# Splitting the last batch's spatial and output products into two 64-row tiles

## The chip, the cores and the metric

The kernel runs on one core of a Trainium2 chip. The time is the device time of one execution in microseconds; the number that counts is the median of several runs. The engines are named as in the profile: PE (TensorE; PEld are its weight loads), DVE (VectorE), ACT (ScalarE), POOL (GpSimd) and SP (SyncE, which issues the DMAs).

## The reference

Causal attention over 4 batches, 12 heads, 448 positions and 64 dimensions, and behind it a gated MLP per batch:

```python
scores = scale * np.matmul(q, k.transpose(0, 1, 3, 2))      # then causal mask, softmax
x = matmul(attn, v) laid out as (batch, 448, 768)
h = gelu(x @ w_in)                                          # 768 -> 1024
u, v = h[..., :512], h[..., 512:]
v_n = (v - mu) / np.sqrt(var + 1e-06) * g_ln
v_s = np.einsum('ts,bsd->btd', w_sg, v_n) + b_sg[None, :, None]
out = x + (u * v_s) @ w_out                                 # 512 -> 768
```

## The kernel before

Attention goes by head pairs, 24 of them, six per batch. For each pair PE computes scores (line 433, plain f32, tiles of 64 rows and 64 columns), DVE masks and finds the maxima (448), ACT takes exponentials (456); then transposes, and the products with v (line 526, tiles of 128 rows and 64 columns). Behind the six pairs of a batch comes `mlp(b)`, whose products are all made by the helper `group` (line 573): it gets a PSUM bank `ps` and a list of weight and moving operands, and issues one matmul each (line 581), in blocks of `CUT` = 3. The operands are of type f32r, split into a high and a low part, so each block of three is high x high, high x low and low x high for one slice of the contraction. All of these matmuls use the full array of 128 rows.

`mlp(b)` has four parts, named in the `od.ctx` keys:

- v: four token tiles, 18 products of 512 columns each (the last tile 12), then gelu, mean and variance, and the normalised `vn` (for the last, half-sized tile `vn3`);
- u: four feature groups of 18 products of 448 columns, gelu into `uT`;
- s: four groups of 11 products of `vn` with w_sg; DVE multiplies by `gcol` and adds `bB` (line 671), POOL multiplies by `uT` (675), ACT and POOL split the result into two halves `gT` (677, 678);
- o: six output groups of 12 products of `gT` with w_out; POOL has put the residual x into `res` (691), DVE adds the bank to it (704) and SP stores it (708 in the last batch, where each group goes out alone and the last one in two halves).

There are eight PSUM banks, shared by everything that PE writes; `bank(tag)` asks for one. Nothing is scheduled at run time: every operation is recorded with a number in `Order.add`, and the table `ORDER` (line 66) is the sequence in which they are written out. Each engine works through its own part of that sequence in order.

Of the kernel before, what the change touches and what calls it, by code (L numbers as in the profile page):

```python
# [13 lines left out]
ALU = mybir.AluOpType  # L14
# [50 lines left out]
FULL = 128, 128  # L65
ORDER = (
# [161 lines left out]
def attention_gated_mlp(ctx: ExitStack, tc: tile.TileContext, qk, vP, w_in, g_ln, w_sgT, b_sg, w_out, out):  # L228
# [338 lines left out]


    vn = {}
    uT = {}  # L570
    gT = {}

    def group(ps, m, n, mms, r):

        per = n / 2400 + (0.02 if n == 512 else 0.0135)
        cut = CUT
        for a in range(0, len(mms), cut):
            def go(a=a):
                for k in range(a, min(a + cut, len(mms))):
# [188 lines left out]
```

## Time and profile before

| | us |
|---|---|
| median of 3 runs | 340.32 (339.68 to 341.67) |
| profiled execution, its own time | 341.12 |
| its span | 339.3 |
| PE busy | 326.6 |
| DVE busy | 258.3 |
| ACT busy | 197.2 |
| POOL busy | 174.1 |

The span is what the profiler sees between the first and the last instruction; the execution's own time holds a little more around it. Matmuls are pipelined, so a matmul's record is longer than the step from one to the next, and the step is read from a run of equal matmuls: its length, less one record, by the number of steps. PEld overlaps PE.

### The profile page before, as it was taken

What the parts mean: (1) busy time and instruction counts of PE and PEld (TensorE: products, weight loads), DVE (VectorE), ACT (ScalarE), POOL (GpSimd) and SP (SyncE); (2) the same over time, 40 slices, a digit from 0 to 9 for tenths busy, and PEclk for the clock granted to TensorE, in tenths of its full rate; (3) what the DMA queues carried; (4) which work ended last, traced back from release to release, by engine and by line L of the source; (5) the groups of instructions that cost most, each with busy time, mean ns of one, the idle gap of its engine ahead of it and who ended that gap; (6) DMA issues with size and microseconds to landing.
All of it is one profiled execution on the core that took longest, in us unless ns stands there. A gap on an engine that the chain in (4) does not pass through costs nothing.

```text
span 339.3 us, 7630 instructions
## 1 busy us (share of the span) xinstructions
PE 326.6 (96%) x2614; PEld 267.5 (79%) x2615; DVE 258.3 (76%) x762; ACT 197.2 (58%) x658; POOL 174.1 (51%) x225
## 2 busy tenths in 40 slices
PE   3999998999999999999999999999999999999994
PEld 2666675868988878878898878877988988889994
DVE  4899976999999988889699767798877521577512
ACT  3999987996667658476645727384645301344300
POOL 4457666787588843223236608402407833352670
PEclk9999999999999999999999999999999999999998
DMA  7887789592584889857769368557342651201003
GB/s 227 321 251 269 251 247 275 150 322 87 126 228 136 243 218 260 231 143 167 174 187 268 101 208 266 111 155 212 83 115 40 209 141 55 108 2 54 0 29 136
DMA packets 31255, 57.75 MB, mean 170 GB/s; under 512 B 3312, under 2 KB 15344, under 8 KB 31216
## 3 DMA queue, kind: packets, MB, share of 16 engines
q1 hardware_dynamic: 31216, 57.26, 58.1%
q8 instruction: 21, 0.34, 0.4%
q14 instruction: 18, 0.15, 0.2%
HBM read 33.39 MB, written 7.08 MB: 119 GB/s over the span
## 4 chain that ended last, share of the span: by engine, by line
PE 83%; ACT 6%; DVE 4%; DMA 4%; issue 1%; SPq 1%; DVEq 0%; ACTq 0%
PE m L581 63%; PE o L526 10%; PE s L433 8%; ACT P L456 5%; DMA rd<-rT 2%; DVE s L448 1%; DMA g<-in_w_out_dram 1%; DMA qk<-in_qk_dram 1%; ACT B L507 1%; ACT vn L368 1%; PE s L470 1%; DVE vn L372 1%; PE tx L500 1%; PE ty L500 1%; DVE vn L370 0%
## 5 line engine op out<-in xcount | busy, mean ns | idle before, releaser
L456 ACT ACTIVATE P<-s,ngm 64x64 f32<-64x64 f32 (+3 forms) x240 | 100.9, 434 | 35.3 <-DVE ngm L448 28.5
L448 DVE CUSTOM_DVE_ANT_0 s<-s,mask 128x192 f32<-128x192 f32 (+3 forms) x192 | 77.2, 438 | 11.2 <-PE s L433 10.0
L581 PE MATMUL m<-win,x 128*128 128x512 f32 (+1 forms) x264 | 65.7, 399 | 0.1
L581 PE MATMUL m<-x,win 128*128 128x448 f32 x288 | 61.5, 367 | 0.0
L581 PE MATMUL m<-g,wout 128*128 128x448 f32 x288 | 61.3, 368 | 0.0
L581 PEld LDWEIGHTS m<-x,win 128*128 128x128 f32 x288 | 53.7, 188 | 5.2
L581 PEld LDWEIGHTS m<-g,wout 128*128 128x128 f32 x288 | 53.5, 188 | 5.1 <-ACT P L456 0.2
L581 PEld LDWEIGHTS m<-win,x 128*128 128x128 f32 (+1 forms) x264 | 46.7, 183 | 11.9 <-POOL win L375 0.2
L433 PE MATMUL s<-qk 64*64 64x64 f32 (+5 forms) x768 | 46.6, 375 | 6.4 <-DMA qk<-in_qk_dram 5.1
L456 ACT ACTIVATION_READ_ACCUMULATOR P<-s,ngm 128x1 f32 (+1 forms) x240 | 49.9, 208 | 0.0
L433 PEld LDWEIGHTS s<-qk 64*64 64x64 f32 x768 | 30.4, 140 | 23.4 <-issue 10.1
L526 PE MATMUL o<-B,vraw 128*64 128x64 f32 (+4 forms) x672 | 45.3, 291 | 0.3 <-DVE B L505 0.3
L526 PEld LDWEIGHTS o<-B,vraw 128*64 128x64 f32 x672 | 33.0, 137 | 13.5 <-issue 5.5
L488 DVE STREAM_TRANSPOSE P<-P 128x1024 f32<-128x1024 f32 x32 | 38.9, 1228 | 2.1 <-DMA B<-P 1.8
L691 POOL TENSOR_TENSOR res<-x 128x448 f32<-128x448 f32 x24 | 27.6, 1166 | 21.5 <-DMA out_dram<-res 21.3
L581 PE MATMUL m<-wsg,vn 128*128 128x448 f32 x176 | 38.1, 367 | 0.0
L562 POOL TENSOR_TENSOR x<-xt,x 128x448 fp32r<-128x448 f32 x24 | 27.5, 1148 | 15.2 <-ACT x L561 14.9
L581 PEld LDWEIGHTS m<-wsg,vn 128*128 128x128 f32 x176 | 32.7, 188 | 2.9
L704 DVE TENSOR_TENSOR res<-m,res 128x448 f32<-128x448 f32 (+1 forms) x25 | 14.7, 600 | 19.0 <-PE m L581 19.0
L592 ACT ACTIVATE tmp<-tmp 128x448 f32<-128x448 f32 (+2 forms) x32 | 18.9, 601 | 16.4 <-DVE tmp L590 16.4
L625 POOL TENSOR_TENSOR mv<-mv,mhalf 128x1 f32<-128x1 f32 (+1 forms) x16 | 10.0, 626 | 35.8 <-DVE mv L623 35.7
L675 POOL TENSOR_TENSOR tmp<-tmp,g 128x448 f32<-128x448 f32 x16 | 18.3, 1148 | 17.5 <-DVE tmp L671 17.4
(77 smaller groups left out, 395.2 us busy)
## 6 DMA issues: line engine op xcount, KB each, us to landing
B<-P SPq DMA_DIRECT2D x64, 256.0 KB
qk<-in_qk_dram SPq DMA_DIRECT2D x24, 448.0 KB
vn<-in_w_in_dram SPq DMA_DIRECT2D x12, 512.0 KB
vraw<-in_vP_dram SPq DMA_DIRECT2D x24, 256.0 KB
rb<-rd SPq DMA_DIRECT2D x24, 224.0 KB
out_dram<-res SPq DMA_DIRECT2D x9, 448.0 KB
g<-in_w_out_dram SPq DMA_DIRECT2D x16, 192.0 KB
rd<-rT SPq DMA_DIRECT2D x48, 32.0 KB
```

The source lines that it names most:

```text
L433: nc.tensor.matmul(out=s[z][bk].t[64 * h:64 * h + 64, col:col + n], lhsT=qk_.t[r, 0, q0:q0 + 64], rhs=qk_.t[r, 1, k0:k0 + n], start=True, ...
L448: nc.vector.tensor_tensor_reduce(out=o, in0=i, in1=mk, scale=-0.125, scalar=3e38, op0=ALU.add, op1=ALU.min, accum_out=ngm[ib[z]][c][0:m])
L456: act(n, lambda c=c, m=m, k0=k0, n=n, bk=bk, col=col, off=off, kc=kc, i=i, z=z: nc.scalar.activation(out=P[i][0:m, off:off + n], in_=s[z][ ...
L488: dve(PW, lambda z=z: nc.vector.transpose(A[ia][:, :, :, z, :].rearrange("p g t k -> p t g k"), P[ib[z]]), Pk[z] + [kp], Ak, 1.105)
L526: nc.tensor.matmul(out=dst(o.t[r]), lhsT=vr.t[:, c, r], rhs=src(z), start=first and n == 0, stop=last and n == len(lst) - 1)
L562: pool_tt(S, lambda: nc.gpsimd.tensor_tensor(out=y.t[:, S + 64:], in0=x.t, in1=f(y.t)[:, 0:S], op=ALU.subtract), [x, y], [(y, 1)])
L581: nc.tensor.matmul(out=ps.t[0:l().shape[1], 0:n], lhsT=l(), rhs=rr(), start=(k == 0), stop=(k == len(mms) - 1))
L592: act(n, lambda: nc.scalar.activation(out=z(), in_=z(), func=AF.Tanh, scale=GS * GC), [], [t], True)
L625: od.add("pool", 0.46, lambda mv=mv, m=m: nc.gpsimd.tensor_tensor(out=mv.t[0:m, 1:2], in0=mv.t[0:m, 1:2], in1=mhalf[0:m], op=ALU.pow), ["s ...
L675: pool_tt(S, lambda z=z, u=u: nc.gpsimd.tensor_tensor(out=z(), in0=z(), in1=u.t, op=ALU.mult), [u], [t])
L691: pool_tt(S, lambda rr=rr, x=x, k=k: nc.gpsimd.tensor_tensor(out=rr.t[:, k, :], in0=f(x.t)[:, 0:S], in1=f(x.t)[:, S + 64:], op=ALU.add), [ ...
L704: dve(hi - lo, lambda rr=rr, ps=ps, z=z, lo=lo, hi=hi: nc.vector.tensor_tensor(out=rr.t[:, z, lo:hi], in0=ps.t[:, lo:hi], in1=rr.t[:, z, l ...
```

## The change

Only in the last batch (`b == B - 1`), the s groups and five of the six o groups get a second PSUM bank `ps2`. `group` then issues each product as two matmuls: rows 0 to 63 of both operands into `ps`, rows 64 to 127 into `ps2`, each in its own row tile. The sums of the two banks are brought together by DVE: in an s group the old instruction reads `ps`, and a second one of the same kind adds `ps2` times `gcol`; in an o group an additional add takes `ps2` into `res` ahead of the old one. The sixth o group is left whole. The added operations give new numbers, and the table `ORDER` is another one throughout.

```diff
+    378, 390, 76, 385, 77, 341, 379, 719, 724, 726, 725, 79, 734, 467, 399, 732, 727, 495, 736, 759, 760, 765, 763,
...
-    def group(ps, m, n, mms, r):
+    def group(ps, m, n, mms, r, ps2=None):
...
                     l, rr = mms[k]
-                    nc.tensor.matmul(out=ps.t[0:l().shape[1], 0:n], lhsT=l(), rhs=rr(), start=(k == 0), stop=(k == len(mms) - 1))
+                    for o, h in ((ps, slice(0, 128)),) if ps2 is None else ((ps, slice(0, 64)), (ps2, slice(64, 128))):
+                        nc.tensor.matmul(out=o.t[0:l().shape[1], 0:n], lhsT=l()[h], rhs=rr()[h], start=(k == 0),
+                                         stop=(k == len(mms) - 1))
...
-            pe(per * len(mms[a:a + cut]), go, rd, [ps])
+            pe(per * len(mms[a:a + cut]), go, rd, [ps] + [ps2] * (ps2 is not None), FULL if ps2 is None else (64, 128))
...
         for dc in range(FC):
-            ps = bank("m")
+            ps, ps2 = bank("m"), bank("m") if b == B - 1 else None
             od.ctx = ("s", b, dc)
...
-            group(ps, 128, S, mms, r)
+            group(ps, 128, S, mms, r, ps2)
...
                 out=z(), in0=ps.t[:, 0:S], scalar=gcol[:, dc:dc + 1], in1=bB, op0=ALU.mult, op1=ALU.add),
                 [ps, "gb"], [t])
+            if ps2 is not None:
+                dve(S, lambda z=z, ps2=ps2, dc=dc: nc.vector.scalar_tensor_tensor(
+                    out=z(), in0=ps2.t[:, 0:S], scalar=gcol[:, dc:dc + 1], in1=z(), op0=ALU.mult, op1=ALU.add),
+                    [ps2, "gb"], [t])
...
         for mc in range(KC):
-            ps = bank("m")
+            ps, ps2 = bank("m"), bank("m") if b == B - 1 and mc < KC - 1 else None
...
-            group(ps, 128, S, mms, r)
+            group(ps, 128, S, mms, r, ps2)
...
+            if ps2 is not None:
+                dve(S, lambda rr=rr, ps2=ps2, z=z: nc.vector.tensor_tensor(
+                    out=rr.t[:, z, :], in0=ps2.t[:, 0:S], in1=rr.t[:, z, :], op=ALU.add), [ps2], [(rr, z)])
```

What stands where, at three places. First PE in the last batch, where the products with w_sg begin. In the names, `x` and `win` are a u group, `wsg` and `vn` an s group. In the kernel before, blocks of the two kinds alternate:

```order
L581 MATMUL m_3736<-x_3636,win_87 128x448 x3
L581 MATMUL m_3740<-x_3509,win_87 128x448 x3
L581 MATMUL m_3740<-x_3511,win_87 128x448 x3
L581 MATMUL m_3740<-x_3631,win_87 128x448 x3
L581 MATMUL m_3843<-wsg_89,vn_3680 128x448 x3
L581 MATMUL m_3740<-x_3636,win_87 128x448 x3
L581 MATMUL m_3747<-x_3511,win_87 128x448 x3
```

In the kernel after, on the same engine at the same place:

```order
L582 MATMUL m_3833<-x_3494,win_87 128x448 x3
L582 MATMUL m_3833<-x_3600,win_87 128x448 x3
L582 MATMUL m_3833<-x_3636,win_87 128x448 x3
L582 MATMUL m_3854<-wsg_89,vn_3685 128x448
L582 MATMUL m_3856<-wsg_89,vn_3685 128x448
```

All u groups now stand ahead of the first s group, and from there the two banks (3854 and 3856) take turns, call by call, through the s groups and five o groups; the last o group, with full products, stands at the end.

Second DVE in the last batch, from the last s groups to the first output adds; `tmp` is the gated value, `res` the output. Before:

```order
L671 SCALAR_TENSOR_TENSOR tmp_3922<-m_3843,gcol_84,bB_85 128x448
L671 SCALAR_TENSOR_TENSOR tmp_3934<-m_3907,gcol_84,bB_85 128x448
L704 TENSOR_TENSOR res_3678<-m_3943,res_3678 128x448
L704 TENSOR_TENSOR res_3997<-m_3959,res_3997 128x448
L704 TENSOR_TENSOR res_3684<-m_3951,res_3684 128x448
```

After:

```order
L673 SCALAR_TENSOR_TENSOR tmp_3963<-m_3925,gcol_84,bB_85 128x448
L677 SCALAR_TENSOR_TENSOR tmp_3963<-m_3927,gcol_84,tmp_3963 128x448
L673 SCALAR_TENSOR_TENSOR tmp_3977<-m_3933,gcol_84,bB_85 128x448
L677 SCALAR_TENSOR_TENSOR tmp_3977<-m_3935,gcol_84,tmp_3977 128x448
L710 TENSOR_TENSOR res_4058<-m_3983,res_4058 128x448
L713 TENSOR_TENSOR res_4058<-m_3981,res_4058 128x448
L710 TENSOR_TENSOR res_4060<-m_3999,res_4060 128x448
```

Each result now takes two instructions, one for each bank, back to back.

Third the first loads on SP at the start of the program; `qk` is a pair's q and k, `vn` here a staging tile for a chunk of w_in, `vraw` a pair's v. Before:

```order
L426 DMA qk_162<-in_qk_dram 128x896
L366 DMA vn_201<-in_w_in_dram 128x1024
L426 DMA qk_207<-in_qk_dram 128x896
L366 DMA vn_254<-in_w_in_dram 128x1024
L366 DMA vn_257<-in_w_in_dram 128x1024
L426 DMA qk_282<-in_qk_dram 128x896
```

After:

```order
L426 DMA qk_155<-in_qk_dram 128x896
L426 DMA qk_176<-in_qk_dram 128x896
L366 DMA vn_211<-in_w_in_dram 128x1024
L366 DMA vn_214<-in_w_in_dram 128x1024
L366 DMA vn_216<-in_w_in_dram 128x1024
L520 DMA vraw_218<-in_vP_dram 128x512
```

The second pair's q and k moved ahead of the first chunk of w_in. On ACT the first exponentials correspondingly stand ahead of the first weight split, and one of the warm-up matmuls (line 341) stands ahead of the first scores on PE, where before all seven stood among the transposes.

## Rows read from the trace of the kernel before

**Rows 1.** The page, busy time, share of the span, instructions of each engine:

```profile
PE 326.6 (96%) x2614; PEld 267.5 (79%) x2615; DVE 258.3 (76%) x762; ACT 197.2 (58%) x658; POOL 174.1 (51%) x225
```

**Rows 2.** The table by stretches: length, busy time by engine, granted clock, DMA:

```profile
core 0: us, PE busy (x) PEld busy (x) DVE busy (x) ACT busy (x) POOL busy (x), PEclk, DMA share, GB/s
0.00:30.00 30.00, 23.76 (x236) 16.14 (x238) 23.43 (x101) 24.28 (x92) 16.12 (x41) 1.00 0.83 269
30.00:60.00 30.00, 27.82 (x290) 19.62 (x288) 24.45 (x101) 26.66 (x102) 19.53 (x24) 1.00 0.83 256
...
270.00:300.00 30.00, 30.00 (x187) 25.29 (x186) 10.18 (x20) 5.24 (x9) 12.27 (x15) 1.00 0.30 86
300.00:310.00 10.00, 10.00 (x51) 9.22 (x50) 7.57 (x14) 4.21 (x8) 4.55 (x5) 1.00 0.13 48
310.00:320.00 10.00, 10.00 (x51) 9.27 (x50) 7.04 (x13) 4.18 (x9) 3.96 (x4) 1.00 0.00 0
320.00:330.00 10.00, 10.00 (x51) 9.26 (x50) 1.45 (x3) 1.72 (x3) 8.93 (x8) 1.00 0.07 25
330.00:339.30 9.30, 5.03 (x25) 4.32 (x23) 3.10 (x6) 0.00 (x0) 0.00 (x0) 0.90 0.35 124
```

**Rows 3.** The chain that ended last, its end: start, length, what:

```profile
281.17 53.88 PE m L581 x257
...
335.14 0.39 DVE res L704
```

**Rows 4.** The timeline of PE, two places: start, length, operation, records:

```profile
251.79 1.99 PE L581 MATMUL m<-wsg,vn 128*128 128x448 f32 x9
253.71 1.76 PE L433 MATMUL s<-qk 64*64 64x448 f32 x32
255.40 3.75 PE L526 MATMUL o<-B,vraw 128*64 128x256 f32 x64
259.08 1.08 PE L581 MATMUL m<-wsg,vn 128*128 128x448 f32 x4
...
320.27 14.76 PE L581 MATMUL m<-g,wout 128*128 128x448 f32 x72
```

**Rows 5.** Groups by shape, 281.2 to 335 us: count | busy, mean ns | idle before:

```profile
L581 PE MATMUL m<-g,wout 128*128 128x448 f32 x81 | 17.1, 365 | 0.0
...
L581 PEld LDWEIGHTS m<-g,wout 128*128 128x128 f32 x81 | 15.2, 188 | 1.3
...
L704 DVE TENSOR_TENSOR res<-m,res 128x448 f32<-128x448 f32 x8 | 4.9, 620 | 10.2 <-PE m L581 10.2
L675 POOL TENSOR_TENSOR tmp<-tmp,g 128x448 f32<-128x448 f32 x4 | 4.6, 1154 | 4.8 <-DVE tmp L671 4.8
L678 POOL TENSOR_TENSOR g<-tmp,g 128x448 fp32r<-128x448 f32 x4 | 4.6, 1154 | 0.7 <-ACT g L677 0.7
...
L671 DVE SCALAR_TENSOR_TENSOR tmp<-m,gcol,bB 128x448 f32<-128x448 f32 x4 | 2.7, 682 | 2.9 <-PE m L581 2.9
...
L677 ACT ACTIVATE g<-tmp 128x448 fp32r<-128x448 f32 x4 | 2.3, 578 | 5.1 <-POOL tmp L675 5.1
...
L581 PEld LDWEIGHTS m<-win,x 128*64 128x64 f32 x6 | 0.8, 134 | 0.3
```

**Rows 6.** The page, costliest groups, scores: matmuls and weight loads of the whole run:

```profile
L433 PE MATMUL s<-qk 64*64 64x64 f32 (+5 forms) x768 | 46.6, 375 | 6.4 <-DMA qk<-in_qk_dram 5.1
...
L433 PEld LDWEIGHTS s<-qk 64*64 64x64 f32 x768 | 30.4, 140 | 23.4 <-issue 10.1
```

**Rows 7.** Who waited for whom in the first 62 us: total, times, longest:

```profile
PE s L433 <- DMA qk<-in_qk_dram: 5.1, 2, 3.9
...
DVE g L370 <- DMA g<-in_w_out_dram: 1.8, 2, 1.4
```

**Rows 8.** The timeline of ACT at the start:

```profile
0.72 1.28 ACT L368 ACT_TABLE_LOAD   x1 [0.72 <-PEq L757]
7.00 0.67 ACT L368 ACTIVATE vn<-vn 128x512 f32<-128x512 f32 x1 [5.00 <-DMA vn<-in_w_in_dram]
```

183 rows, old and new, of the table ORDER are left out of this document.

## The prediction

> **What bounds the kernel now.** I read the summary first: TensorE (PE) is busy 326.6 us of a 339.3 us span, far ahead of VectorE (DVE) with 258.3 [rows 1]. Then the table by stretches, to see where PE is not full: it lacks 6.2 us in the first 30 us and 2.2 us in the next 30; from 270 to 330 it is full; then it stops [rows 2]. DVE in the last batch is the reverse: 7.04 of 10 us, then 1.45 of 10. The chain that ended last says the same: from 281.17 us on it is one piece of 53.88 us, PE products of line 581, and behind it the last add on DVE [rows 3]. So in the last batch a microsecond taken from PE is a microsecond of the kernel, and work given to DVE is free while it stays off the tail. In the first 56 us PE waits, and there other engines decide; I come back to them.
>
> **The products.** 72 products of 448 columns in a row took 14.76 us [rows 4]. A record outlives the start of the next product, so I take one record (365 ns [rows 5]) off and divide by the 71 steps: (14.76 - 0.365)/71 = 0.203 us per product. The granted clock there is 1.00, the 2.4 GHz level [rows 2]; 448 columns at one column a cycle are 187 ns. So 16 ns of each product are not streaming.
>
> The Trainium skill, page "TensorE: Matmul & The Clock Gate", section "Back-to-back issue gap", gives N/2.4 + 2.5 ns for one warm product, here 189 ns. The trace has 203 for the full array. If the pairs of the change ran at the page's figure, the saving below would be 104 x 14 = 1.4 us and the sum 339.2.
>
> **What the change does to them.** 44 products with w_sg and 60 of the 72 with w_out become pairs: 104 pairs, each two calls of 64 rows into two banks. First question: do the two run side by side? In before the score calls (line 433) are tiles of 64 rows and 64 columns; 32 records that average 375 ns [rows 6] took 1.76 us together [rows 4], about seven at a time, where the 72 full products, at 365 ns, are 1.8 at a time. Their 768 weight loads of 140 ns sum to 107.5 us and took 30.4 us of busy time [rows 6], 3.5 at a time. So tiles of half the rows do run and load beside each other, in another type (plain f32, not f32r).
>
> Second question: what does a pair cost? No row shows f32r in 64-row tiles, so I bound it. Low end: streaming alone, 187 ns. High end without any trouble: 203, if the 16 ns belong to the type and not to the shape. Between lie the tiled calls of line 526: 64 records, two heads side by side, so 32 steps (two pairs, 1024 columns a head, two records a call), 4096 columns at two cycles each = 3.41 us, took 3.75 us [rows 4]; 0.17 us of it is the last record's overhang (a product's record is 365 - 203 = 162 ns longer than its step), which leaves (3.75 - 3.41 - 0.17)/32 = 5 ns a step. I take 187 + 5 = 192 ns, because these are the nearest tiled calls; saving 104 x 0.011 = 1.14 us, bounds 0 and 1.66.
>
> **Entering and leaving the tiles.** The order after puts all u groups ahead of the first w_sg product and the unsplit sixth output group last, so the mode changes twice. From full products to score tiles: nine products from 251.79 should end their steps at 253.62, the scores start at 253.71, 0.09 us [rows 4]. From line 526 back to products: 255.40 + 3.41 + 32 x 0.005 = 258.97, the products start at 259.08, 0.11 us [rows 4]. Two changes, 0.2 us.
>
> **DVE, POOL and banks.** DVE gains four adds of 0.68 and five of 0.62 us [rows 5], 5.8 us, against 2.96 + 8.55 + 6.20 = 17.7 us idle after 310 [rows 2]. What hides them must be checked by place, so I lay the after order out with these durations, counting pairs of 0.192 us from the first w_sg product (time 0). Group s0 ends at pair 11, 2.1; with 0.2 us to start, its two DVE instructions end at 3.7. POOL then has eight instructions of 1.15 us with ScalarE's 0.58 between the first two [rows 5] (behind those POOL itself is the limit), and ends the last gated half at about 14.25. PE first needs that half at pair 76, 14.6. Margin 0.35 us. In DVE's new queue three output adds of the third batch stand ahead of the last token tile's normalisation; one waits for products that end 45 products (9.1 us) after that tile's own, and the first gelu of the u groups and the tile's `vn3` are queued behind it. Going through the queue with the same durations I get `vn3` about 16.1 us after the tile's products; PE needs it 81 products and 9 pairs after them, 18.2 us: no wait. The third output group needs the bank that the second DVE instruction of s2 frees, at about 8.5; it starts at pair 50, 9.6. After POOL come six residual adds taken as equally long, so DVE's adds of output groups two to five queue up and end at about 22.5; the sixth group's products end at 104 x 0.192 + 0.1 + 12 x 0.203 + 0.2 = 22.7. So the tail has the same length, with 0.2 us to spare; the unsplit sixth group keeps its one add in two halves. Cost 0, up to 0.5 us if POOL or DVE is a little late. If these margins go, what is late next is the DVE add in front of the last store.
>
> **The rest of the order table.** It is new from the first instruction. What PE does in total is the same, so it counts only where PE waits: 5.1 us for the first two q/k loads and, through DVE, for w_out chunks: DVE waited 1.8 us for them [rows 7]. The new order loads the second q/k tile second and not third, runs the first exponentials before the first weight split on ScalarE, and spreads the first w_out chunks. But ScalarE is busy 24.28 us of the first 30, 1.28 of it the table load, and its first other instruction starts at 7.00 [rows 2, 8]: from there it is full (23.0 of 23.0 us), so an earlier start of one task delays another. I take 0, with 1.8 us either way, the size of the wait that such an order makes or avoids.
>
> **Sum.** The profiled execution took 341.12 us, 1.8 more than its span, and 0.8 more than the median 340.32; differences go onto the median. -1.14 + 0.2 + 0 + 0 = -0.94: 339.4 us.
>
> **Rivals.**
> 1. *The 16 ns belong to f32r.* Then a pair takes 203, the change brings only its two mode changes: 340.32 + 0.2 = 340.5. For it: every full product of the last stretch pays this step, and no tile of that type is in the trace. Against: the f32 tiles step closer. The Trainium skill, page "TensorEngine Tiling (Array Packing)", section "When to Use Tiling", offers row tiling for contractions of up to 64; by it products of 128 rows gain nothing, which is this case.
> 2. *Weight loads of a pair take turns* (slower). A load of 128 columns is 188 ns, of 64 columns 134 [rows 5]: 54 ns per 64, so 108 ns for 128. Two in turn are 215, with the 16 ns 231; per pair +12 to +28 over 203, on 104 pairs 1.2 to 2.9 us, plus 0.2: about 342.6. It decides from 203 + (1.7 - 0.2)/104 = 217 ns a pair. Against it stand the overlapping loads of the score tiles; for it, that those are half as wide. Two whole calls in turn (374 ns) would give 340.3 + 104 x 0.171 + 0.2 = 358; I leave that 2 in 100, within this rival's chance.
> 3. *The new order shortens the start*: the 1.8 us go, 339.4 - 1.8 = 337.6.
> 4. *The new order adds a wait* of that size: 339.4 + 1.8 = 341.2, or 342.3 with rival 1.
>
> **How the numbers follow.** Forecast 0.47, own range 337.9 to 340.9; rival 1 0.18; rival 2 0.13; rival 3 0.14; rival 4 0.08. A measurement of this kernel can tell about 0.5%, 1.7 us, from no change: under 338.6 is faster, over 342.0 slower. Faster: 0.13 of the forecast's share, 0.01 of rival 1, all of rival 3: 0.28. Slower: most of rival 2 (0.11), half of rival 4 and a little of rival 1: 0.18. The same: 0.54. Range 337.3 to 342.7: from just under rival 3 to rival 2.
>
> **What would show it.** In the profile after: pairs of line 582 in the last batch with a step near 0.192 us (203 speaks for rival 1, over 215 for rival 2) and starts of the two calls a few ns apart; weight loads of the two halves overlapping; PE without a gap from the first pair to the last product; the last DVE add starting about 0.1 us after PE ends; the waits for q/k and w_out in the first 62 us against 5.1 and 1.8 us. The forecast is wrong if the pair's step is not shorter than a product's, or if the stretch before the last batch moves by more than the last batch does.

## The result, and the profile after

The changed kernel took 344.0 us (median of four runs, 343.9 to 344.15) against 340.28 of the kernel before: a ratio of 1.0104, interval 1.0073 to 1.0135. It is 1% slower, outside the forecast range of 337.3 to 342.7. The profiled execution took 344.15 us with a span of 342.4, so 3.0 us more than the profiled execution of before.

The page of the changed kernel, busy time, share of the span and instructions, answers to [rows 1]:

```profile
PE 329.8 (96%) x2719; PEld 267.0 (78%) x2719; DVE 266.2 (78%) x771; ACT 197.2 (58%) x658; POOL 175.0 (51%) x225
```

TensorE became 3.2 us busier by this count, VectorE 7.9 us. The table by stretches (length, then busy time of each engine, granted clock, DMA) answers to [rows 2]:

```profile
core 0: us, PE busy (x) PEld busy (x) DVE busy (x) ACT busy (x) POOL busy (x), PEclk, DMA share, GB/s
0.00:30.00 30.00, 24.52 (x218) 14.22 (x220) 22.81 (x102) 22.80 (x87) 15.33 (x39) 1.00 0.83 284
30.00:60.00 30.00, 29.24 (x311) 20.99 (x308) 26.33 (x102) 29.14 (x107) 22.57 (x29) 1.00 0.79 242
60.00:90.00 30.00, 29.55 (x214) 23.65 (x213) 28.90 (x83) 24.26 (x78) 22.40 (x28) 1.00 0.65 203
...
150.00:180.00 30.00, 28.20 (x219) 22.84 (x216) 27.01 (x60) 13.87 (x41) 13.31 (x14) 1.00 0.57 154
...
270.00:300.00 30.00, 30.00 (x187) 25.21 (x186) 12.75 (x25) 5.95 (x10) 11.59 (x14) 1.00 0.25 70
300.00:335.00 35.00, 35.00 (x274) 32.89 (x275) 19.98 (x37) 10.24 (x18) 19.11 (x19) 1.00 0.07 27
```

In the kernel before, TensorE was full in two of these stretches:

```profile
60.00:90.00 30.00, 30.00 (x220) 24.38 (x219) 29.05 (x89) 24.98 (x78) 23.20 (x29) 1.00 0.61 186
150.00:180.00 30.00, 30.00 (x247) 25.41 (x244) 25.84 (x65) 16.43 (x48) 10.76 (x12) 1.00 0.66 167
```

In the last batch, where the tiles are, TensorE is as full as before. It is no longer full between 60 and 90 us (0.45 us missing) and between 150 and 180 us (1.80 missing). The waits of TensorE, over the whole run, give the names (who waited for whom: total, times, longest), against [rows 7]:

```profile
PE m L341 <- DVE tmp L336: 2.1, 1, 2.1
PE m L582 <- DVE xt L553: 1.6, 1, 1.6
PE s L433 <- DMA qk<-in_qk_dram: 1.3, 1, 1.3
...
PE s L470 <- DVE rs L467: 0.7, 2, 0.4
```

The q/k wait fell from 5.1 to 1.3 us, but there is a new wait of 2.1 for the warm-up's operand at line 341. The wait for `xt` of 1.6 us is new, and it lies at 177 us.

For a finer view I weighted every matmul with its step (0.203 us for a product of 448 columns, half of that for each call of a pair, 0.227 for 512 columns, and so on) and compared the moments at which TensorE has begun the same amount of work. The lag behind the profiled execution of before, in us, at moments of the kernel before:

| moment (us) | 76.5 | 84.6 | 101.1 | 168.2 | 184.8 | 307.9 | 333.9 |
|---|---|---|---|---|---|---|---|
| changed kernel | -0.45 | -0.45 | 0.72 | 0.60 | 2.95 | 3.08 | 3.48 |

So of 3.9 us, 1.2 are lost around 85 to 100 us, 2.3 between 168 and 185 us, and 0.4 in the last batch. (The profiled execution of before lost about 0.9 us in its first 50 us that other executions of the same order did not: two runs below, which share its order there, stand at -0.86 and -0.89 at 76.5 us. The changed kernel's start at -0.45 is therefore no gain, but 0.4 behind them.)

**The pairs.** The timeline of TensorE in the last batch (start, length, operation, records) and the groups by shape after 316 us (count | busy, mean ns) answer to [rows 4] and [rows 5]:

```profile
314.52 9.17 PE L582 MATMUL m<-wsg,vn 64*128 64x448 f32 x88
323.52 15.00 PE L582 MATMUL m<-g,wout 64*128 64x448 f32 x132
```

```profile
L582 PE MATMUL m<-g,wout 64*128 64x448 f32 x120 | 12.3, 362 | 0.0
L582 PEld LDWEIGHTS m<-g,wout 64*128 64x128 f32 x120 | 11.7, 185 | 0.5
```

88 records are 44 pairs. 9.17 less one record (0.362) is 8.81 us from the first start to the last, 43 steps of 0.205; without the tenth of a microsecond that the entry takes, 0.2025. Within a pair the two calls start 10 ns apart, from one pair to the next pass 193: side by side as forecast, but in the time of one full product, 203 ns, not 192.

**The long step.** VectorE's timeline at 171 us, where the lag jumps (start, length, line, operation, what the idle time before waited for):

```profile
171.51 3.87 DVE L629 TENSOR_SCALAR tmp<-tmp,mv 64x512 f32<-64x512 f32 x1 [0.52 <-POOL mv L627]
...
175.84 0.27 DVE L471 COPY rT<-s 8x128 f32<-8x128 f32 x1
...
177.96 0.62 DVE L553 TENSOR_TENSOR xt<-o,rb 128x448 f32<-128x448 f32 x1
178.61 0.68 DVE L640 TENSOR_TENSOR vn<-tmp,vn 64x512 fp32r<-64x512 f32 x1
```

and GpSimd's timeline in the same microseconds:

```profile
170.93 0.54 POOL L627 TENSOR_TENSOR mv<-mv,mhalf 64x1 f32<-64x1 f32 x1 [1.95 <-ACT tmp L591]
171.45 1.14 POOL L562 TENSOR_TENSOR x<-xt,x 128x448 fp32r<-128x448 f32 x1
172.56 0.32 POOL L564 TENSOR_TENSOR x<-xt,x 128x64 fp32r<-128x64 f32 x1
172.83 2.26 POOL L697 TENSOR_TENSOR res<-x 128x448 f32<-128x448 f32 x2
```

The step that normalises the fourth token tile of batch 1 (line 629; line 627 in the kernel before) takes 3.87 us. Its group shows what is usual (min/median/max in ns):

```profile
L629 DVE TENSOR_SCALAR tmp<-tmp,mv x16: 505/540/3866, 70.1 to 312.2; 128x512 f32<-128x512 f32 x12, 64x512 f32<-64x512 f32 x4
```

It starts 0.06 us after GpSimd's L562 and ends 0.29 us after GpSimd's last of four instructions without a gap (172.83 + 2.26 = 175.09). Behind it on VectorE stand the transposed sums `rT` (L471), the `xt` of L553 that TensorE then waits 1.6 us for, and the tile's `vn3` half (L640). A smaller case stands near 82 us: L629 1.54 us and L372 1.30 us beside GpSimd's instructions, and TensorE waits for the reciprocal (L467) behind them.

### The profile page after: what moved, and what is told of

It reads as the page before. It is cut to its first block, busy times and chain, and to the rows that moved or that the text cites. A ratio compares the mean times of both kernels' runs of the same rounds, so it can differ in the third digit from the quotient of the medians.

```text
span 342.4 us, 7860 instructions
## 1 busy us (share of the span) xinstructions
PE 329.8 (96%) x2719; PEld 267.0 (78%) x2719; DVE 266.2 (78%) x771; ACT 197.2 (58%) x658; POOL 175.0 (51%) x225
## 4 chain that ended last, share of the span: by engine, by line
PE 77%; DVE 7%; ACT 6%; DMA 4%; issue 2%; SPq 2%; POOL 1%; DVEq 0%; POOLq 0%; ACTq 0%
PE m L582 54%; PE o L526 10%; PE s L433 9%; ACT P L456 4%; SPq L492 2%; PE ty L500 2%; PE tx L500 2%; DMA B<-P 1%; DVE P L488 1%; DVE s L448 1%; DMA rb<-rd 1%; POOL tmp L681 1%; DMA qk<-in_qk_dram 1%; ACT vn L368 1%; PE s L470 1%
## 5 line engine op out<-in xcount | busy, mean ns | idle before, releaser
L448 DVE CUSTOM_DVE_ANT_0 s<-s,mask 64x64 f32<-64x64 f32 (+3 forms) x192 | 76.6, 440 | 8.8 <-PE s L433 6.6
L582 PE MATMUL m<-g,wout 128*128 128x448 f32 (+1 forms) x348 | 62.5, 368 | 0.0
L582 PEld LDWEIGHTS m<-g,wout 128*128 128x128 f32 (+1 forms) x348 | 53.9, 187 | 5.2 <-issue 0.3
L456 ACT ACTIVATION_READ_ACCUMULATOR P<-s,ngm 128x1 f32 (+1 forms) x240 | 51.4, 216 | 0.0
L433 PE MATMUL s<-qk 64*64 64x64 f32 (+5 forms) x768 | 48.2, 371 | 2.2 <-DMA qk<-in_qk_dram 1.3
L582 PE MATMUL m<-wsg,vn 128*128 128x448 f32 (+1 forms) x220 | 39.1, 370 | 1.8 <-DVE xt L553 1.6
L582 PEld LDWEIGHTS m<-wsg,vn 128*128 128x128 f32 (+1 forms) x220 | 32.5, 187 | 6.4 <-DVE xt L553 2.3
L562 POOL TENSOR_TENSOR x<-xt,x 128x448 fp32r<-128x448 f32 x24 | 27.5, 1148 | 12.8 <-ACT x L561 12.5
L627 POOL TENSOR_TENSOR mv<-mv,mhalf 128x1 f32<-128x1 f32 (+1 forms) x16 | 9.3, 582 | 39.1 <-DVE mv L625 23.8
L635 POOL TENSOR_TENSOR vn<-tmp,vn 128x512 fp32r<-128x512 f32 x12 | 15.9, 1328 | 24.0 <-ACT vn L634 24.0
```

The lines of the kernel that those rows point to most:

```text
L433: nc.tensor.matmul(out=s[z][bk].t[64 * h:64 * h + 64, col:col + n], lhsT=qk_.t[r, 0, q0:q0 + 64], rhs=qk_.t[r, 1, k0:k0 + n], start=True, ...
L448: nc.vector.tensor_tensor_reduce(out=o, in0=i, in1=mk, scale=-0.125, scalar=3e38, op0=ALU.add, op1=ALU.min, accum_out=ngm[ib[z]][c][0:m])
L456: act(n, lambda c=c, m=m, k0=k0, n=n, bk=bk, col=col, off=off, kc=kc, i=i, z=z: nc.scalar.activation(out=P[i][0:m, off:off + n], in_=s[z][ ...
L562: pool_tt(S, lambda: nc.gpsimd.tensor_tensor(out=y.t[:, S + 64:], in0=x.t, in1=f(y.t)[:, 0:S], op=ALU.subtract), [x, y], [(y, 1)])
L582: nc.tensor.matmul(out=o.t[0:l().shape[1], 0:n], lhsT=l()[h], rhs=rr()[h], start=(k == 0), stop=(k == len(mms) - 1))
L635: pool_tt(DH, lambda y=y, z=z: nc.gpsimd.tensor_tensor(out=y.t[:, 1, :], in0=z(), in1=f(y.t)[:, 0, :], op=ALU.subtract), [t, y], [(y, 1)])
```

## The experiments

My theory after this reading was that the order table is the loss and the tiles only a few tenths; the rival was that the tiles cost the time. In the diffs of orders, the rows are instructions in the sequence in which their engine issues them.

### Tiles without the new order, the order without tiles, and a control

```diff
- ORDER of the changed kernel
+ ORDER of the kernel before up to the last u product of the last batch,
+ then the changed kernel's order from the first w_sg product of the last batch on
```

> The changed kernel's code with the two-tile products of the last batch, but every instruction up to the last input product of the last batch in the order of the kernel before; only the tail from the first w_sg product of the last batch on stands in the changed kernel's order. Theory A (the loss of 3 us in TensorE's work up to 180 us of the span comes from the new order table, the tiles themselves save nothing and cost 0.1 to 0.5 us): 340.4 to 340.9 us, ratio to before 1.000 to 1.002. Rival B (the tiles cost the time, and the lag seen at 180 us is only waiting that would have come later anyway): 343.5 to 344.3, ratio 1.010.

Measured: 341.67 us, ratio 1.0056 (1.0040 to 1.0072).

```diff
- ps, ps2 = bank("m"), bank("m") if b == B - 1 else None
+ ps = bank("m")
  ORDER of the changed kernel, without the nine added additions
```

> The kernel before, without tiles and without the nine added VectorE additions, issued in the changed kernel's order. Theory A (the order is the loss): 343.3 to 344.1 us, ratio 1.009 to 1.011, with VectorE's normalising step of about 3.9 us near 171.5 us again. Rival B (the tiles are the loss): 340.0 to 340.6, ratio 1.000.

Measured: 343.59 us, ratio 1.0109 (1.0091 to 1.0127). The long step is there again in VectorE's timeline (line numbers of the experiments' kernels are up to six off those of the changed kernel):

```profile
171.63 3.87 DVE L626 TENSOR_SCALAR tmp<-tmp,mv 64x512 f32<-64x512 f32 x1 [0.52 <-POOL mv L624]
```

The control has the sequence of the first of these runs, without tiles:

> Control for the first run: the kernel before without tiles, with the tail from the first w_sg product of the last batch on in the changed kernel's order and everything ahead of it as before. It prices the regrouped tail alone. Theory A: 340.1 to 340.6 us, ratio 0.999 to 1.001; the difference of the first run to it is the price of the tiles with their nine additions, 0 to 0.5 us. Rival B: 340.3 as well, with the first run 3.5 us above it.

Measured: 341.23 us, ratio 1.0037 (1.0014 to 1.0060).

The order alone gives 3.4 of the 3.7 us. By the medians the tiles cost 344.0 - 343.59 = 0.41 us in the new order and 341.67 - 341.23 = 0.44 in the old one, but the intervals of each two runs overlap, so these differences alone do not show it. The traces do: from 307.9 to 333.9 us the lag grows by 0.40 us in the changed kernel and by 0.01 in its order without tiles. Both runs with the old order came out above what I expected, by 0.8 and 0.6 us: the tail put behind the old order is not free. In the control's lag 0.46 us arise in the tail (from -0.50 at 307.9 us to -0.04 at the end), where a weight load waits 0.37 us at 312.8 us for the last token tile's `vn3`. In the first run 1.29 arise there: 0.4 are the mode changes below, and weight loads wait 0.5 us for the second bank's VectorE instruction (L677) and 0.4 for GpSimd's L684, waits that the changed kernel's own order does not have. So the difference of these two runs is no clean price of the tiles. Another 0.46 arise between 185 and 193 us, where the order is that of the kernel before; the first run, with the same order there, does not have them, so I count them as spread.

### Is it GpSimd's run of instructions?

```diff
  POOL L562 x<-xt,x   pair 12
  POOL L564 x<-xt,x
- POOL L697 res<-x
- POOL L697 res<-x
  POOL L562 x<-xt,x   pair 13
+ POOL L697 res<-x
+ POOL L697 res<-x
```

> The changed kernel with GpSimd's two additions for the second batch's output (1.1 us each, near 173 us) moved behind its next residual difference, so that GpSimd's run beside VectorE's normalising step of the fourth token tile is two instructions (1.46 us) and not four (3.7 us). Theory C (VectorE's step can't start its work until GpSimd's run of instructions ends, and TensorE waits for what stands behind it): the step falls from 3.87 us to 1.4 to 1.9, TensorE's lag at 180 us falls by 1.5 to 2.4 us, total 341.6 to 342.5. Rival D (the step is long for another reason, such as its own inputs, or the tensor engine would lose the time elsewhere): 343.7 to 344.3.

Measured: 341.72 us, ratio 1.0048 (1.0036 to 1.0060), 2.3 us less than the changed kernel. Timelines of VectorE and GpSimd:

```profile
171.62 1.36 DVE L629 TENSOR_SCALAR tmp<-tmp,mv 64x512 f32<-64x512 f32 x1 [0.52 <-POOL mv L627]
...
171.56 1.14 POOL L562 TENSOR_TENSOR x<-xt,x 128x448 fp32r<-128x448 f32 x1
172.67 0.49 POOL L564 TENSOR_TENSOR x<-xt,x 128x64 fp32r<-128x64 f32 x1
```

Two instructions of GpSimd that share no data with the step were moved, and the lag at 184.8 us fell from 2.95 to 0.73. Now VectorE gets in between L562 and L564, and it is L564 that becomes longer (0.49 for 0.32).

The next two ask what in the run counts. In the first, only one of the two additions is moved; in the second the additions stand ahead of L562 and L564.

> The changed kernel with only the second of the two GpSimd additions moved behind the next residual difference: GpSimd's run beside VectorE's normalising step near 171.5 us is three instructions (1.14 + 0.32 + 1.15 us). Theory C1 (VectorE's step waits for the whole run): it takes 2.6 to 2.8 us, total 342.2 to 343.2. Theory C2 (it waits for one instruction only, unless exactly this run of four stands there): 1.3 to 1.5 us, total 341.5 to 342.0. Rival D (the run has nothing to do with it): 3.87 us and 344.

> The changed kernel with the same four GpSimd instructions in another order: the two additions (1.15 us each) first, then the residual difference of 448 columns and the one of 64. Theory C1 (length of the run decides): the VectorE step takes 3.6 to 3.9 us again, total 343.5 to 344.5. Theory C2' (what decides is which instruction stands next; beside two of these additions in a row near 161 us a step took 1.37 us): 1.3 to 1.6 us, total 341.5 to 342.5, a part of which may be lost again because the residual difference comes 2.3 us later.

Measured: 343.12 us (ratio 1.0084, 1.0060 to 1.0107) and 343.81 us (1.0115, 1.0092 to 1.0138). VectorE and GpSimd with the run of three:

```profile
171.72 2.76 DVE L629 TENSOR_SCALAR tmp<-tmp,mv 64x512 f32<-64x512 f32 x1 [0.53 <-POOL mv L627]
...
173.04 1.15 POOL L697 TENSOR_TENSOR res<-x 128x448 f32<-128x448 f32 x1
```

and with the additions first:

```profile
171.40 3.58 DVE L629 TENSOR_SCALAR tmp<-tmp,mv 64x512 f32<-64x512 f32 x1 [0.53 <-POOL mv L627]
...
171.34 2.24 POOL L697 TENSOR_TENSOR res<-x 128x448 f32<-128x448 f32 x2
173.55 1.15 POOL L562 TENSOR_TENSOR x<-xt,x 128x448 fp32r<-128x448 f32 x1
174.66 0.50 POOL L564 TENSOR_TENSOR x<-xt,x 128x64 fp32r<-128x64 f32 x1
```

2.76 us for three, 3.58 and 3.87 for four: the step grows with the run, in either order of the four, and ends 0.28 to 0.29 us after one of its instructions. TensorE's loss goes with it: between 168.2 and 184.8 us the lag grows by 0.01 us beside the run of two, by 1.33 beside three, and by 2.05 and 2.35 beside four. After which instruction VectorE gets in is not the same everywhere. With the additions first it gets in ahead of the last one (L564 is again the longer, 0.50), in the run of two after the first, and in the run of three and in the changed kernel only after the last. Beside the two additions in a row at 160.96 us of the changed kernel it got in after the first (its step took 1.37 us). What decides that stays open.

### Another form of the same step

```diff
+ acc = (b, tcn) == (1, 3)
  nc.vector.tensor_scalar(out=z(), in0=z(), scalar1=..., scalar2=...,
-     op0=ALU.subtract, op1=ALU.mult)
+     op0=ALU.subtract, op1=ALU.mult, **(dict(accum_out=st.t[0:m, 0:1]) if acc else {}))
```

> The changed kernel in its own order, GpSimd's run of four untouched; only VectorE's normalising step of the fourth token tile of the second batch (the one of 3.87 us) is issued in the form that also writes a running result to a spare column, so that it is no longer the plain two-constant form. If the long step is a matter of the port that the plain form and GpSimd's instructions both need (the Trainium skill, page SBUF - State Buffer, section Who interferes with whom, excepts the form with accumulator output): the step takes 0.5 to 0.8 us, total 341.3 to 342.2. If GpSimd's run holds up any VectorE step there, or the step waits for a signal from GpSimd: 3.5 to 3.9 us, total 343.7 to 344.3.

Measured: 341.77 us, ratio 1.0053 (1.0032 to 1.0074); in this form the values of that one token tile are not the reference's normalisation. GpSimd's run of four was unchanged. VectorE and GpSimd:

```profile
171.61 0.80 DVE L630 TENSOR_SCALAR_CACHE_REDUCE tmp<-tmp,mv 64x512 f32<-64x512 f32 x1 [0.53 <-POOL mv L627]
172.34 0.07 DVE L630 DVE_READ_ACCUMULATOR tmp<-tmp,mv 64x1 f32 x1
...
171.55 1.15 POOL L562 TENSOR_TENSOR x<-xt,x 128x448 fp32r<-128x448 f32 x1
172.66 0.32 POOL L564 TENSOR_TENSOR x<-xt,x 128x64 fp32r<-128x64 f32 x1
172.94 2.27 POOL L698 TENSOR_TENSOR res<-x 128x448 f32<-128x448 f32 x2
```

0.80 us instead of 3.87, beside the same four instructions at the same moment. So it is neither the data nor a signal from GpSimd that the step waits for; the plain form needs something that GpSimd's run holds, and the other form doesn't. The Trainium skill, page "SBUF — State Buffer", section "Who interferes with whom", names it as the port pair of the state buffer that VectorE and GpSimd share: `tensor_scalar` can enter a two-port mode in which it contends with GpSimd, the form that also writes out its accumulator does not, and whoever issues first holds the pair for its whole instruction while the other is blocked. The trace agrees on the form (0.80 against 3.87) and, beside a run of two, on the length of the block (1.36: the rest of L562 and 0.28). Where the page has one instruction to wait for, the runs of three and four show 2.76 and 3.87 us; there the measurement decides. No row here names a port, so that it is the port rests on the page; that the plain form is held and the other is not is measured.

### The reverse: the run in the kernel before

```diff
- POOL L691 res<-x
...
- POOL L562 x<-xt,x
  POOL L625 mv<-mv,mhalf
+ POOL L562 x<-xt,x
+ POOL L564 x<-xt,x
  POOL L691 res<-x
+ POOL L691 res<-x
- POOL L564 x<-xt,x
```

> The reverse test: the kernel before, in its own order but for GpSimd, where near 172 us the same four instructions (residual difference of 448 columns and of 64, then the two additions) now stand behind the small power instruction that VectorE's normalising step of the fourth token tile waits for. Theory C (a run of GpSimd instructions holds the step, and TensorE waits for what stands behind it): the step, 1.36 us in the kernel before, takes 2.5 to 3.9 us, and the total rises by 1 to 2.5 us to 341.3 to 342.8. Rival (the loss needs the rest of the changed kernel's order): 340.0 to 340.6.

Measured: 341.42 us, ratio 1.0034 (1.0014 to 1.0054). VectorE and GpSimd in the kernel before:

```profile
172.96 1.36 DVE L627 TENSOR_SCALAR tmp<-tmp,mv 64x512 f32<-64x512 f32 x1
...
172.90 1.14 POOL L691 TENSOR_TENSOR res<-x 128x448 f32<-128x448 f32 x1
```

and with the run:

```profile
171.84 2.74 DVE L627 TENSOR_SCALAR tmp<-tmp,mv 64x512 f32<-64x512 f32 x1
...
170.64 1.16 POOL L562 TENSOR_TENSOR x<-xt,x 128x448 fp32r<-128x448 f32 x1
171.76 0.31 POOL L564 TENSOR_TENSOR x<-xt,x 128x64 fp32r<-128x64 f32 x1
172.04 2.25 POOL L691 TENSOR_TENSOR res<-x 128x448 f32<-128x448 f32 x2
```

The step doubles from 1.36 us, and again ends 0.29 us after the run. TensorE's lag rises by 1.3 us (from -1.02 at 168.2 us to 0.28 at the end), but only 0.7 of it arise right behind the step, at 176 to 178 us. The other 0.5 arise at 188 us, where the control without the run lost 0.46 too, so I do not count them. For the long step and a part of the loss the mechanism needs nothing else of the new order; here VectorE reaches the step 1.2 us after the run began, and so waits for less of it.

### The second place, and the price of the tiles once more

```diff
  POOL L635 vn<-tmp,vn   batch 0
  POOL L376 win<-vn,win
- POOL L697 res<-x
  POOL L375 wout<-g
...
  POOL L376 wout<-g,wout
+ POOL L697 res<-x
```

Together with the move of the two additions above:

> The changed kernel with the two GpSimd additions of the fourth experiment moved, and also the one near 82.6 us (first output group of batch 0) moved behind the weight casts near 95 us, since VectorE's weight step took 1.30 us beside it (0.34 elsewhere) and TensorE then waited 1.0 us for the reciprocal of the softmax sums. Theory C: TensorE's wait at 85 us falls from 1.0 to 0 to 0.2 us, total 340.6 to 341.1. Rival (the time is lost again further on, where the addition now stands or in the next wait): 341.5 to 341.9.

Measured: 340.32 us, ratio 1.0012 (1.0000 to 1.0025). In the run with only the two additions moved, TensorE, VectorE and GpSimd stood like this:

```profile
86.00 0.27 PE L470 MATMUL s<-ident,rs 128*8 128x128 f32 x1 [0.88 <-DVE rs L467]
...
83.27 1.31 DVE L372 SCALAR_TENSOR_TENSOR g<-g 128x192 int32<-128x192 int32 x1
...
83.02 1.34 POOL L697 TENSOR_TENSOR res<-x 128x448 f32<-128x448 f32 x1
```

With the third addition moved as well, TensorE no longer waits at 84.8 us, and VectorE's L372 takes 0.35 us:

```profile
84.78 0.27 PE L470 MATMUL s<-ident,rs 128*8 128x128 f32 x1
...
82.65 0.35 DVE L372 SCALAR_TENSOR_TENSOR g<-g 128x192 int32<-128x192 int32 x1
```

It gave 1.4 us where I had expected 0.6 to 1.1. The lag between 84.6 and 101.1 us, 1.6 us in the run with only the two additions moved, is gone as a whole, and not only the wait of 0.88 that the profile names there. The same order without tiles:

> The kernel before, without tiles, in the changed kernel's order with the three GpSimd additions moved (the order of the run with both moved). It gives the price of the tiles once more, in an order without the two long holds: 0.3 to 0.8 us below 340.32, so 339.5 to 340.0, which would be 0 to 0.2% below the kernel before. Rival (the tiles cost nothing here): 340.3.

Measured: 339.91 us, ratio 0.9982 (0.9965 to 0.9998): the lowest median of all, about 0.2% below the kernel before. The two runs with the three additions moved were not taken beside the same executions of the kernel before (medians 340.05 and 340.32), so the difference of their medians, 340.32 - 339.91 = 0.41 us, is a rough one; by the two ratios it is about 1 us. The traces are closer: in the last batch the lag grows by 0.40 us with the tiles and by 0.01 without, as in the first comparison.

### The step of a product, by type and shape

```diff
- mms.append((lambda y=y, a=a, d=d: y.t[:, a, d], lambda c=c, l=l: wsg[:, c, l, :]))
+ mms.append((lambda y=y, a=a, d=d: h16(y.t, (a,), d, b == B - 1),
+             lambda c=c, l=l: h16(wsg, (c, l), slice(0, S), b == B - 1)))
+ def h16(t, i, d, bf):
+     i = (slice(None),) + i
+     if not bf:
+         return t[i + (d,)]
+     return t.bitcast(BF16)[i + (slice(2 * d.start + 1, 2 * d.stop, 2),)]
```

> The changed kernel with the last batch's products on the upper halves of the same words read as bf16: w_sg products as two 64-row tiles as in the changed kernel, output groups as full products with one bank (the values differ from the reference's there, and the five second additions are left out). It measures the step without the fp32r type. If the 16 ns beyond the 187 ns of streaming belong to the type (rival 1 of the prediction): full products and pairs both step 188 to 192 ns. If they belong to a full-array product (the forecast): full 200 to 205, pairs 188 to 193. If the pair itself costs a full step whatever the type: both 200 to 205. A read with a stride that is slower would show as a step above 205 in both.

Measured, TensorE's timeline:

```profile
314.19 8.86 PE L588 MATMUL m<-wsg,vn 64*128 64x448 bf16 x88
322.99 14.38 PE L588 MATMUL m<-g,wout 128*128 128x448 bf16 x72
```

With one record (0.355 and 0.358) taken off: (14.38 - 0.358)/71 = 0.1975 us for a full product and (8.86 - 0.355)/43 = 0.198 for a pair. None of the three expectations fits as written. In bf16 pair and full product have the same step (0.198), and so they have in f32r (0.203): the shape counts for nothing. The type accounts for 5.5 of the 16 ns beyond streaming; the other 10 may belong to the read of every second word or to something else, which this run doesn't separate. A row of the kernel before bears on it, which I had overlooked. Its warm-up is seven bf16 products of 512 columns on the full array, read without a stride (one record is missing):

```profile
17.67 1.67 PE L341 MATMUL m<-tmp 128*128 128x512 bf16 x6
```

One record (0.378) taken off, (1.67 - 0.378)/6 = 0.215 us, 2 ns over the 213 of streaming, where an f32r product of 512 columns steps 0.227. So a full-array product does not by itself cost 16 ns.

## Why the prediction was wrong

**The step that failed.** It is the one on the rest of the order table, that the new order "counts only where PE waits": 0, with 1.8 us either way. By itself the new order cost 3.4 us, by waits that it makes where TensorE had none: 2.3 us behind VectorE's normalising step held by GpSimd's run near 171 us, and 1.4 near 82 us. The rest of the order gains about 0.3 (2.3 + 1.4 against 3.4). Two smaller terms were mis-sized beside it, the pair's gain and the mode changes. Both signs of being wrong that the prediction named came true: the pair's step is not shorter, and the stretch ahead of the last batch moved by 3.1 us (the lag at 307.9), the last batch by 0.4. To a time over 342.0 I had given 0.18.

**What bounds the kernel.** Right for TensorE: from 60 us on it had no wait in the kernel before. The step on the order failed by this very fact. In a stretch without waits an order has no wait to remove, but it can make one, and there was 270 us of room for that. I took the bound of 1.8 us from the waits of the start [rows 7]. The start, which I did weigh, gave nothing: the q/k wait is 3.8 us shorter, but 2.1 are new at the warm-up, and by the lag at 76.5 us the start stands 0.4 us behind the runs with the old order.

**What I had not looked at.** I laid out VectorE's and GpSimd's queues for the last batch alone, and gave each instruction its usual duration. The stretch from 60 us to the last batch I did not lay out at all. The trace of before held a warning in the group of the same step (min/median/max in ns):

```profile
L627 DVE TENSOR_SCALAR tmp<-tmp,mv x16: 507/546/1631, 68.2 to 311.4; 128x512 f32<-128x512 f32 x12, 64x512 f32<-64x512 f32 x4
```

The three that took over 1.3 us, at 172.96, 236.70 and 303.68 us, stood beside a GpSimd instruction that began within 0.1 us of them. Four GpSimd instructions in a row behind the one that releases the step could be read from the order. Their price of 2.3 us could not be read from any row of before, where no such step had more than one long instruction to wait for, but the direction could.

**The pair's step.** Forecast 192 ns with bounds 187 and 203; measured 203. The tiled calls of line 526 that I took as the nearest row said nothing about it. Rival 1 was right in its number and, as far as the runs go, in its reason: the 16 ns do not belong to the shape, for pairs gain nothing over full products in f32r or in bf16. How much of them is the type itself stays open. The warm-up's full-array products, 2 ns over streaming in the kernel before, spoke against giving the 16 ns to the shape. The term of -1.14 us is 0. (The side sum of the prediction with a saving of 1.4 us comes to 339.1, not 339.2.)

**The mode changes.** Forecast 0.2 us for both; they cost 0.4, which is all that the tiles cost in the last batch's lag. The steps across the two changes in the trace of the changed kernel show it: entering, two successive pair starts lie 297 and 309 ns after the one before instead of 203; leaving, the first full product starts 294 ns after the last call instead of 193 and the second 308 after it instead of 207. That is 0.2 us each, twice what I had read at the score tiles [rows 4]: I had taken one late step at each change, and there are two.

**VectorE, GpSimd, banks and the tail.** Right. TensorE is without a gap from the first pair to the last product, the nine added VectorE additions hide behind it, and the last addition starts with the end of TensorE as before. None of the margins of 0.2 to 0.35 us was used up; with a pair's step of 203 ns instead of 192 they were also wider than I had reckoned.

**The rivals.** Rival 2 did not occur: the loads of a pair, 185 ns each, overlap. Rival 3 did not. What happened is rival 1 together with rival 4, which I had priced at 342.3; rival 4's mechanism was a wait that the new order makes, with a chance of 0.08 and a price of 1.8 us. Both were too small. With the measured terms the sum closes: 340.2 + 3.4 (order) + 0.4 (tiles) = 344.0.

## What to carry to other kernels

When a change brings a new order, go through it on each pair of engines that can block each other, not only through the waits of before: a long run of GpSimd instructions right behind the signal that releases a VectorE step is a cost, even where the two share no data. An order that leaves TensorE no slack shows no wait in its trace, and still has everything to lose. And before you put a product's extra time down to its shape, look for a row with the same shape in another type. Two half-height calls side by side took the time of one full product, in two types, so splitting the contraction bought nothing by itself.

## What the runs showed of the hardware that was not expected

- VectorE's two-constant step of 512 columns, 0.51 to 0.55 us alone, took 1.36, 2.76, 3.58 and 3.87 us beside runs of two, three, four and four GpSimd instructions. In the form with accumulator output it took 0.80 beside the run that made it 3.87.
- VectorE operations with two inputs, both in SBUF, were held too, though not for as long: in the changed kernel L372 took 1.30 us for 0.35 and L596 1.28 for 0.68, each beside one GpSimd instruction.
- 64-row pairs into two banks start 10 ns apart in f32r and 3 ns apart in bf16, and step like one full product: 203 and 198 ns at 448 columns.
- Each change between full products and pairs cost 0.2 us in f32r, over two steps. In the bf16 run it was about 0.1, nearly all in one step.
